# Causal attention with a channel mix: masks added after the score products, chunks 0 and 2 in one group, full-array spreads, a new order of all engines

## The chip, the cores and the metric

The kernel runs on one core of a Trainium2 chip. TensorE (PE in the rows, its weight loads PEld) multiplies matrices and writes to PSUM, VectorE (DVE), ScalarE (ACT) and GpSimd (POOL) do the elementwise work, and SyncE (SP) issues the transfers (DMA). The metric is the time of one execution on the device in microseconds, lower is better. The kernel before takes 474.48 us, the median of three runs (474.12 to 476.29).

## What is computed

Causal attention over 4 batches of 12 heads (448 positions, 64 values per head), then a channel mix on the joined heads (768 channels, 1024 inside):

```
scores = scale * q @ k.T ; scores[upper triangle] = -1e9
attn   = exp(scores - max) / (sum + 1e-9)
x      = (attn @ v) of all 12 heads side by side           # 4 x 448 x 768
xk = mu_k * x + (1 - mu_k) * x_prev ; xr = mu_r * x + (1 - mu_r) * x_prev
out = sigmoid(xr @ w_r) * (max(xk @ w_k, 0)**2 @ w_v)
```

`x_prev` is x one position earlier, zero at the start.

## The kernel before, in words

Two heads lie side by side on the 128 partitions: a pair w. There are 24 pairs, six to a batch. The 448 positions are cut into four chunks of 112. For chunk c of the queries, only keys up to chunk c are needed, so a row of scores has 112*(c+1) columns. The tiles of PSUM that hold scores (`s`, two buffers) hold several chunks: a **group** g, listed in `STEPS` (L389): chunks 0 and 1, chunk 2, chunk 3.

For one pair, in this order: `score` (L391) first writes the mask of the diagonal block into the group, as four matmuls of the identity `pick` with the triangle `mask` (L405; two halves h of a diagonal block, for two heads j), then adds the products of q and k (L418). The first six pairs multiply in full f32; from pair 6 on (`short`), q and k are split into a rounded part and a rest (`qk_hi`, `qk_lo`: tiles qh and ql), and three faster products are summed. The two heads j use rows 0 to 63 and 64 to 127 of the array, at the same time. `row_max` (L435, DVE) takes each row's maximum, one instruction for each chunk, `row_top` (L449 on DVE or L447 on ACT) turns it into a bias, `exps` (L458, ACT) takes the exponentials e and their sums. The weights e are then transposed: on TensorE for the first batch (`turn_e` L663, copied out by `copy_e` L674), later as two f16 parts p (`prob_hi` L639, `prob_lo` L643), turned by a DMA into pT. `weighted` (L705) multiplies them with v into the tile `bank`; this uses 64 columns of the array at a time. The reciprocals of the sums go through `turn_r` (L616) and `spread` (L626), and `evac` (L722) multiplies both into x. `mix_now`, `mix`, `mix_hi`, `mix_lo` (L249 to L255, L749, L756, L760) make xk and xr.

When six pairs are done, the batch's channel mix follows on TensorE: `mk` (xk times w_k, 8 outputs of 6 steps), `mr` (xr times w_r, 6 of 6) and `mv` (6 of 8), 448 columns at a time. For batch 0, mk and mr are full f32 matmuls (L981, two passes each, which the trace shows as two MATMULs); for the others a step is three f16 matmuls (L966). While one batch is mixed, the attention of the next one runs between its steps. For each batch some numbers are needed that are the largest over all partitions: `across` (L263) turns a column into a row (`turn`, tiles tp, L270), takes the maximum on DVE (`most`), and multiplies a 1x1 or 2x2 diagonal, tile `dg`, with a weight of ones to spread it to all partitions (`spread`, tiles bp, L281). The weight of this matmul has as many rows as numbers: 1 or 2. There are ten such spreads.

The three weight matrices come as 64-bit numbers, which are put together from two 32-bit halves: `w_z` (ACT, L840) reads the high half, `w_top` (POOL or ACT, L848, L850) the low one, `w_bits` (DVE, L854) joins them.

What runs in which order is written out by hand: each piece of work is a `plan.op`, and the table `starts` has a rank for every op; all instructions are issued in order of rank, so each engine's queue is in that order. The table `engines` says where an op that could run on ACT, DVE or POOL does run. `fills` puts matmuls into TensorE's queue whose result nothing uses (`idle`, L298), a pair of them for each unit, so many at this and that rank. An engine executes its queue in order; it waits for what an instruction needs.

The lines that the change touches:

Of the kernel before, what the change touches and what calls it, by code (L numbers as in the profile page):

```python
# [22 lines left out]
UP = 2.0**14  # L23
# [77 lines left out]
def tile_causal_attention_channel_mix(  # L101
# [73 lines left out]
    nc.vector.tensor_copy(pick[:D, 0], ident[:D, :CP])  # L175
    nc.vector.tensor_copy(pick[D:, 0, :D], ident[D:, D:])
    nc.vector.tensor_copy(pick[:D, 1, D:], ident[:D, : CP - D])
    nc.vector.tensor_copy(pick[D:, 1, D:], ident[D:, D:CP])
    nc.vector.tensor_copy(mask[:D], mask_up[:D])
    ident_h = const.tile([P, P], F16, name="identh")  # L180
# [22 lines left out]
    if "T" in CHOICE["pv"]:  # L203
        ident_b = early.tile([P, P], BF16, name="identb")
        nc.gpsimd.tensor_copy(ident_b, ident)
        mask_t = early.tile([P, 2, 1, CP], BF16, name="maskt")
        maskt_up = parted(x_ts[-2][:, 1 : 1 + CP])
        cleared(mask_t, maskt_up)
        triangles(mask_t, maskt_up, [[-D, 2], [0, 1], [1, CP]], -1, 0, masked)
        nc.vector.tensor_copy(mask_t[:D], maskt_up[:D])  # L210
        sel_m = early.tile([3 * N8, N8], BF16, name="selm")
        nc.gpsimd.memset(sel_m, 0.0)
        for i in range(3):
            nc.gpsimd.affine_select(
                out=sel_m, in_=sel_m, pattern=[[-1, N8]], compare_op=ALU.not_equal,
                fill=1.0, base=-N8 * i, channel_multiplier=1,
            )
        hot = early.tile([CP, NCH + 32], F32, name="hot")
        nc.gpsimd.memset(hot, 0.0)
        nc.gpsimd.memset(hot.rearrange("p (a c) -> p a c", c=NCH)[:, :, NCH - 1 :], 1.0)  # L220
        sel_t = early.tile([D, NCH, 2, D], F16, name="selt")
        nc.gpsimd.memset(sel_t, 0.0)
        nc.gpsimd.affine_select(
            out=sel_t, in_=sel_t, pattern=[[-1, NCH], [-32, 2], [0, D]], compare_op=ALU.not_equal,
            fill=1.0, base=0, channel_multiplier=1,
        )
        log_up = early.tile([P, 1], F32, name="logup")
        nc.gpsimd.memset(log_up, LOG_UP)
# [107 lines left out]

    def scaled_v(b, pv):
        s = p2.tile([P, 2], F32, tag="vsc", name=f"vsc_{b}")
        nc.vector.reciprocal(s[:, 0:1], pv)
        nc.vector.tensor_scalar(s[:, 1:2], s[:, 0:1], UP, None, ALU.mult)  # L340
        vsc[b] = (pv, s[:, 1:2])
        if plain(b, "k") and plain(b, "r"):
            nc.vector.tensor_scalar(shares_h, shares_p, pv, 1.0 / UP, ALU.mult, ALU.mult)

    def whole_p(w):

        return CHOICE["pv"][w] in "FT"

    def flipped(w):
        return CHOICE["pv"][w] == "T"  # L350
# [21 lines left out]
    def parts_v(w, i, e):  # L372
        s = vsc[w // NPAIR][1][:CP]
        src = vraw[w]
        if i == 0:
            vs[w] = p2.tile([CP, 2, 2 * NCH, D], F16, tag="vs", name=f"vs_{w}", bufs=NVS)
            scaled(vs[w][:, 0], src, s, e)
        elif e == "D":
            nc.vector.scalar_tensor_tensor(  # L379
                vs[w][:, 1], src, s, vs[w][:, 0], ALU.mult, ALU.subtract  # L380
            )
        else:
            scaled(src, src, s, e)
            tt[e](vs[w][:, 1], src, vs[w][:, 0], ALU.subtract)

    vmm, em, stat, sps, tot, sm = {}, {}, {}, {}, {}, {}


    STEPS = [{0: 0, 1: CP}, {2: 0}, {3: 0}]  # L389

    def score(w, g):  # L391

        s = ps_s.tile([P, 2, 512], F32, tag="s", name=f"s_{w}_{g}")
        sps[w, g] = s
        for h in range(2):
            for j in range(2):
                rows = slice(D * j, D * j + D)
                a = D * h
                if g == 0:
                    diagonal = s[:CP, j, :S].rearrange("p (a b) -> p a b", a=2)[:, :, a:CP]  # L400
                    fill = mask[rows, h, :, a:].to_broadcast([D, 2, CP - a])
                else:
                    (c,) = STEPS[g]
                    diagonal, fill = s[:CP, j, CP * c + a : CP * (c + 1)], mask[rows, h, 0, a:]
                nc.tensor.matmul(  # L405
                    diagonal, pick[rows, h], fill, start=h == 0, stop=False, skip_group_check=True
                )
# [31 lines left out]
    def most(w, g, a, z):  # L439
        a0 = min(STEPS[g])  # L440
        return sps[w, g][:CP, 0, S + 2 * (a - a0) : S + 2 * (z - a0)].rearrange("p (c j) -> p c j", j=2)
# [1097 lines left out]
```

## Time and profile before

| | |
|---|---|
| median of three runs | 474.48 us |
| the profiled execution's own time | 474.86 us |
| its span, first to last instruction | 473.1 us |
| granted TensorE clock, mean | 0.998 of full speed |
| busy: TensorE, DVE, ACT, POOL | 459.8, 353.8, 297.5, 178.3 us |

The span is 1.8 us shorter than the execution's time, for what lies before the first and after the last instruction. The table of stages (below) cuts the span at four places: the start of the first mk step (64.3 us), the last long wait of TensorE for ScalarE (118.4), and the start of the second batch's mk (193.6).

### The profile page before, as it was taken

The page shows a single profiled execution, that of the slowest core. Times are in us where ns is not written, and L with a number is a line of the kernel's source. Part 1 is how long each engine was busy: PE and PEld are TensorE (multiplying, and loading weights), DVE is VectorE, ACT ScalarE, POOL GpSimd, SP SyncE. Part 2 cuts the span into 40 slices and gives each one's busy share as a digit, 9 for nine tenths or more (in the row PEclk, how much of TensorE's full clock was granted, in tenths as well). Part 3 has the DMA queues.
Part 4 walks back from the last instruction along what each step waited for, and adds up shares of the span by engine and source line. Part 5 has one row for each costly group of instructions (what it writes and reads, how often), then busy time and mean ns, then how long its engine had stood idle before and what let it go on. Part 6 is the DMA issues. An engine that isn't in the chain of part 4 may idle for free.

```text
span 473.1 us, 9479 instructions
## 1 busy us (share of the span) xinstructions
PE 459.8 (97%) x3601; PEld 269.2 (57%) x3601; DVE 353.8 (75%) x722; ACT 297.5 (63%) x817; POOL 178.3 (38%) x177
## 2 busy tenths in 40 slices
PE   7989899999999899999999999999999999999996
PEld 5667655555465565555565666555665655555553
DVE  5899999898899988978797788775767784253211
ACT  5989889999949677578667544284578451223200
POOL 4424534414100433345323674237564542028200
PEclk9999999999999999999999999999999999999999
DMA  8787938573136658475156398363078673000002
GB/s 270 275 331 253 327 112 241 209 177 88 41 66 114 150 84 175 131 168 130 39 118 115 73 184 199 94 149 87 2 99 138 137 133 92 1 0 1 0 21 98
DMA packets 94846, 60.59 MB, mean 128 GB/s; under 512 B 83408, under 2 KB 86480, under 8 KB 94032
## 3 DMA queue, kind: packets, MB, share of 16 engines
q1 hardware_dynamic: 94800, 59.98, 50.5%
q8 instruction: 28, 0.46, 0.4%
q14 instruction: 18, 0.15, 0.1%
HBM read 33.82 MB, written 5.51 MB: 83 GB/s over the span
## 4 chain that ended last, share of the span: by engine, by line
PE 69%; DVE 4%; ACT 3%; DMA 1%; issue 1%; POOL 0%; DVEq 0%
PE mv L966 20%; PE mk L966 17%; PE mr L966 13%; PE bank L705 5%; PE s L418 5%; PE mr L981 5%; PE s L405 2%; DMA pT<-p 1%; ACT junk L806 1%; PE sp L626 1%; DVE s L435 1%; ACT e L458 1%; DVE vs L379 1%; POOL p L643 0%; DVE ql L369 0%
## 5 line engine op out<-in xcount | busy, mean ns | idle before, releaser
L966 PE MATMUL mv<-k,wv 128*128 128x448 f16 x576 | 113.2, 353 | 0.0
L458 ACT ACTIVATE e<-s,st 112x224 f32<-112x224 f32 (+3 forms) x192 | 92.9, 492 | 15.7 <-DVE st L449 12.3
L966 PEld LDWEIGHTS <-wv 128*128 128x128 f16 x576 | 54.7, 98 | 51.6 <-issue 2.9
L966 PE MATMUL mk<-xk,wk 128*128 128x448 f16 x432 | 83.4, 353 | 0.0
L435 DVE TENSOR_REDUCE s<-s 112x2 f32<-112x224 f32 (+3 forms) x96 | 70.5, 743 | 17.2 <-PE s L418 14.1
L966 PEld LDWEIGHTS <-wk 128*128 128x128 f16 x486 | 46.5, 98 | 44.4 <-issue 2.3
L966 PE MATMUL mr<-xr,wr 128*128 128x448 f16 x270 | 55.4, 353 | 0.0
L643 POOL TENSOR_TENSOR p<-e,p 112x1120 f16<-112x1120 f32 x15 | 36.7, 2447 | 48.2 <-DVE p L639 24.5
L966 PEld LDWEIGHTS <-wr 128*128 128x128 f16 x270 | 25.7, 98 | 23.6 <-issue 0.6
L458 ACT ACTIVATION_READ_ACCUMULATOR e<-s,st 112x1 f32 x192 | 38.9, 203 | 0.0
L981 PE MATMUL mk<-xk,wk 128*128 128x448 f32 x96 | 37.4, 544 | 0.0
L1076 DVE SCALAR_TENSOR_TENSOR a<-mv,kap,a 128x448 f32<-128x448 f32 x24 | 16.2, 678 | 24.7 <-PE mv L966 24.2
L643 DVE TENSOR_TENSOR p<-e,p 112x1120 f16<-112x1120 f32 x21 | 28.9, 1376 | 4.1 <-POOL p L639 3.6
L850 POOL TENSOR_SCALAR wraw<-wraw 128x768 int32<-128x768 uint16 (+1 forms) x19 | 23.3, 1228 | 22.7 <-DMA wraw<-in_w_k_dram 12.6
L705 PEld LDWEIGHTS <-vs 112*64 112x64 f16 x648 | 26.9, 110 | 6.0 <-issue 4.8
L705 PE MATMUL bank<-pT,vs 112*64 112x224 f16 (+1 forms) x648 | 29.7, 245 | 0.5 <-DMA pT<-p 0.5
L981 PE MATMUL mr<-xr,wr 128*128 128x448 f32 x72 | 29.3, 549 | 0.0
L749 DVE SCALAR_TENSOR_TENSOR xf<-xt,shares,xf 128x448 f32<-128x448 f32 x36 | 24.6, 686 | 5.7 <-ACT xf L249 5.4
L981 PEld LDWEIGHTS mk<-xk,wk 128*128 128x128 f32 x96 | 17.8, 190 | 17.4 <-issue 16.3
L639 ACT CAST p<-e 112x1120 f16<-112x1120 f32 x22 | 24.7, 1123 | 4.1 <-DMA pT<-p 4.0
L760 POOL TENSOR_TENSOR xr<-xf,xr 128x448 f16<-128x448 f32 x10 | 12.7, 1270 | 35.8 <-ACT xr L756 21.3
L447 ACT ACTIVATE st<-s 112x2 f32<-112x2 f32 (+1 forms) x37 | 6.2, 171 | 31.4 <-DVE s L435 27.5
(217 smaller groups left out, 850.3 us busy)
## 6 DMA issues: line engine op xcount, KB each, us to landing
qk<-in_qk_dram SPq DMA_DIRECT2D x24, 448.0 KB, 4.2
wraw<-in_w_k_dram SPq DMA_DIRECT2D x6, 1024.0 KB, 6.8
wraw<-in_w_v_dram SPq DMA_DIRECT2D x8, 768.0 KB, 5.2
vraw<-in_v_dram SPq DMA_DIRECT2D x24, 224.0 KB, 4.8
out_dram<-a SPq DMA_DIRECT2D x24, 224.0 KB, 2.4
wraw<-in_w_r_dram SPq DMA_DIRECT2D x6, 768.0 KB, 5.5
pT<-p SPq DMA_TRANSPOSE x36, 4.7
muT<-in_mu_dram SPq DMA_DIRECT2D x1, 6.0 KB, 8.6
```

Source lines behind the costliest of these rows:

```text
L418: nc.tensor.matmul(s[:CP, j, o : o + n], q_[rows, 0, c * CP : (c + 1) * CP], k_[rows, 1, :n], start=False, stop=c == max(STEPS[g]) and i = ...
L435: nc.vector.tensor_reduce(stat[w][:, c, :] if flipped(w) else most(w, g, c, c + 1), s[:CP, :, o : o + CP * (c + 1)], AX.X, ALU.max, negate ...
L458: nc.scalar.activation(em[w, j][:, blocks(c)].rearrange("p a b -> p (a b)"), sps[w, g][:CP, j, o : o + CP * (c + 1)], AF.Exp, bias=stat[w] ...
L639: copy[e](p_t[at_][:, :NB, :CP], em[w, j])
L643: tt[e](p[:, NB:, :CP], em.pop((w, j)), p[:, :NB, :CP], ALU.subtract)
L705: nc.tensor.matmul(px[w][64 * j : 64 * j + 64, cols], value(j, vi), p(j, pi), start=n == 0 and i == 0, stop=last and i == len(steps) - 1, ...
L749: nc.vector.scalar_tensor_tensor(f, x_of(w)[:, :S], share(w, mu, 1), f, ALU.mult, ALU.add)
L760: tt[e](t[:, 1], xf.pop((w, mu)), t[:, 0], ALU.subtract)
L850: nc.gpsimd.tensor_scalar(t, u, TOP3, -0.499, ALU.mult, ALU.add)
L966: nc.tensor.matmul(ps, w[:, wi, cols], x[:, xi, t0 : t0 + n], start=(i == 0 and a == 0), stop=(i == steps - 1 and a == 2),)
L981: nc.tensor.matmul(mps[m, kind, o][:, :n], z[:, o * P : (o + 1) * P], x, start=i == 0, stop=i == NO - 1)
L1076: nc.vector.scalar_tensor_tensor(s, mps.pop((m, "v", o))[:, : M[m][2]], kap[m][:, 3:4], s, ALU.mult, ALU.mult)
```

## The change

The groups become chunk 1; chunks 2 and 0 together; chunk 3. The products come first in a group, and the mask matmuls are added behind them. `pick` gets 128 columns instead of 112 (the last 16 are zero), so a mask matmul now writes all 128 partitions; for that, the first product of a chunk also takes 128 columns of q as its weight (the 16 that lie behind the chunk in memory; nothing reads these rows). In a group of two chunks, the products go chunk by chunk within each of the three summands. `across` multiplies with a weight of ones of all 128 rows; the diagonal lies in one of two tiles of 128x2 that are cleared once. `w_z` and `w_top` are told apart by halves of their tile, so that neither has to come before the other. The code of a way of working that no pair uses (`"T"`, `flipped`) goes. All three tables are new: 2161 ops have another rank, 722 choices of an engine are made anew, and the fills are 87 units instead of 111 (174 matmuls instead of 222, with one more at the start in both).

```
-    "fills": [[5,6],[95,16],[115,3],[255,13],[505,5],[535,4],...
+    "fills": [[15,12],[125,14],[215,9],[525,11],[615,3],[815,2],...
...
-    pick = const.tile([P, 2, CP], BF16, name="pick")
+    pick = const.tile([P, 2, P], BF16, name="pick")
...
+    diag = [const.tile([P, 2], F32, name=f"diag{i}") for i in range(2)]
+    for t in diag:
+        nc.gpsimd.memset(t, 0.0)
...
-            st["dg"] = p2.tile([P, 2], F32, tag="dg", name=f"dg_{nm}")
+            st["dg"] = diag[len(spreads) % 2]
...
-                st["bp"][:, :n], ones[:n].to_broadcast([n, P]), st["dg"][:n, :n], start=True, stop=True
+                st["bp"][:, :n], ones.to_broadcast([P, P]), st["dg"][:, :n], start=True, stop=True
...
-    STEPS = [{0: 0, 1: CP}, {2: 0}, {3: 0}]
+    STEPS = [{1: 0}, {2: 0, 0: 3 * CP}, {3: 0}]
+    PLACE = {c: i for i, c in enumerate(c for g in STEPS for c in g)}
...
-        for h in range(2):
-            for j in range(2):
-                rows = slice(D * j, D * j + D)
-                a = D * h
-                if g == 0:
-                    diagonal = s[:CP, j, :S].rearrange("p (a b) -> p a b", a=2)[:, :, a:CP]
-                    fill = mask[rows, h, :, a:].to_broadcast([D, 2, CP - a])
-                else:
-                    (c,) = STEPS[g]
-                    diagonal, fill = s[:CP, j, CP * c + a : CP * (c + 1)], mask[rows, h, 0, a:]
-                nc.tensor.matmul(
-                    diagonal, pick[rows, h], fill, start=h == 0, stop=False, skip_group_check=True
-                )
...
-        for c, o in STEPS[g].items():
-            n = CP * (c + 1)
-            for i, (q_, k_) in enumerate(products):
+        top = max(STEPS[g])
+        for i, (q_, k_) in enumerate(products):
+            for c, o in STEPS[g].items():
+                n = CP * (c + 1)
                 for j in range(2):
-                    rows = slice(64 * j, 64 * j + 64)
+                    rows = slice(D * j, D * j + D)
+                    wide = P if i == 0 else CP
                     nc.tensor.matmul(
-                        s[:CP, j, o : o + n],
-                        q_[rows, 0, c * CP : (c + 1) * CP],
+                        s[:wide, j, o : o + n],
+                        q_.rearrange("p a s -> p (a s)")[rows, c * CP : c * CP + wide],
                         k_[rows, 1, :n],
-                        start=False,
-                        stop=c == max(STEPS[g]) and i == len(products) - 1,
+                        start=i == 0 and c == top,
+                        stop=False,
                         skip_group_check=True,
                     )
+        for h in (1, 0):
+            for j in range(2):
+                rows = slice(D * j, D * j + D)
+                a, z = D * h, CP * len(STEPS[g])
+                diagonal = s[:, j, CP * top : CP * top + z].rearrange("p (a b) -> p a b", b=CP)[:, :, a:]
+                fill = mask[rows, h, :, a:].to_broadcast([D, len(STEPS[g]), CP - a])
+                nc.tensor.matmul(
+                    diagonal, pick[rows, h], fill, start=False, stop=h == 0, skip_group_check=True
+                )
...
-        plan.op("ACT", scalar(w) + 85, w_z, (n,), [(st, None, "r"), (z, None, "w")])
-        plan.op({"ACT": scalar(w) + 85, "POOL": 1.24 * w + 110}, 0, w_top, (n,), [(st, None, "w")])
+        plan.op("ACT", scalar(w) + 85, w_z, (n,), [(st, "h", "r"), (z, None, "w")])
+        plan.op({"ACT": scalar(w) + 85, "POOL": 1.24 * w + 110}, 0, w_top, (n,), [(st, "l", "w")])
```

On TensorE, a group of one chunk (here chunk 3 of the pair that is scored just ahead of the first mk step) reads before like this, where `s` is the group's tile, and "x2" a matmul for each head:

```order
L405 LDWEIGHTS pick
L405 MATMUL s_2_1156<-mask,pick 112x112
...
L405 MATMUL s_2_1156<-mask,pick 112x48
L418 MATMUL s_2_1156<-ql_1034,qh_1032 112x448 x2
L418 MATMUL s_2_1156<-qh_1032,ql_1034 112x448 x2
L418 MATMUL s_2_1156<-qh_1032 112x448 x2
L981 MATMUL mk_0_1203<-xk_682,wk 128x448
```

On TensorE, a group of chunk 3 of the same pair now (L384 is `score`'s product, L398 its mask):

```order
L384 MATMUL s_2_1070<-ql_999,qh_924 128x448 x2
L384 MATMUL s_2_1070<-qh_924,ql_999 112x448 x2
L384 MATMUL s_2_1070<-qh_924 112x448 x2
L398 LDWEIGHTS pick
L398 MATMUL s_2_1070<-mask,pick 128x48
...
L398 MATMUL s_2_1070<-mask,pick 128x112
```

The four masks have gone behind the products, and the narrower half comes first.

On TensorE, around the first mk steps of batch 0 (xk_682 and so on are the inputs of pairs 0, 1, ...; mk_0, mk_1 outputs), it was:

```order
L418 MATMUL s_2_1156<-qh_1032 112x448 x2
L981 MATMUL mk_0_1203<-xk_682,wk 128x448
L981 MATMUL mk_0_1203<-xk_877,wk 128x448
L981 MATMUL mk_0_1203<-xk_959,wk 128x448
L981 MATMUL mk_0_1203<-xk_1122,wk 128x448
L981 MATMUL mk_0_1203<-xk_1174,wk 128x448
L705 MATMUL bank<-pT_0_1099,vraw_957 64x224
```

On TensorE at the same place (L828 is the f32 step, L463 `turn_r`, L473 `spread`, L510 `turn_e`, L552 `weighted`), now:

```order
L510 MATMUL eT_1_2_1092<-ident,e_1_889 112x112 x4
L463 LDWEIGHTS rs_136
L463 MATMUL rp_1101<-identh,rs_136 128x112
L828 MATMUL mk_0_1103<-xk_585,wk 128x448
L828 MATMUL mk_0_1103<-xk_697,wk 128x448
L828 MATMUL mk_1_1120<-xk_585,wk 128x448
L828 MATMUL mk_1_1120<-xk_697,wk 128x448
L473 LDWEIGHTS sel
L473 MATMUL sp_1128<-rt_1125,sel 128x112
```

The mix starts when the inputs of two pairs are there, with two outputs at a time; eleven steps, not five, stand ahead of the next pair's scores, among the last steps of pairs 4 and 5.

On DVE, the first reductions of the program (s_0 is pair 0's first group; "x2" is two instructions, L179 the end of the mask's making) were:

```order
L179 COPY mask<-xt_95 64x224
L435 TENSOR_REDUCE s_0_171<-s_0_171 112x2 x2
L435 TENSOR_REDUCE s_1_187<-s_1_187 112x2
L449 TENSOR_SCALAR st_180<-s_1_187 112x2
L435 TENSOR_REDUCE s_2_242<-s_2_242 112x2
```

On DVE at the start of the program (L410 `row_max`, L423 `row_top`), now:

```order
L179 COPY mask<-xt_95 64x224
L410 TENSOR_REDUCE s_0_189<-s_0_189 112x2
L423 TENSOR_SCALAR st_196<-s_0_189 112x2
L410 TENSOR_REDUCE s_1_204<-s_1_204 112x2 x2
L423 TENSOR_SCALAR st_196<-s_1_204 112x4
```

The first group has one reduction where it had two, and the second one two.

## Rows read from the trace of the kernel before

**Rows 1.** Busy time by stage: start:end, length, each engine's busy us (instructions), clock, DMA.

```profile
0.00:64.30 64.30, 57.87 (x702) 41.53 (x702) 54.77 (x114) 54.53 (x169) 28.94 (x47) 1.00 0.80 276
64.30:118.40 54.10, 53.10 (x244) 28.33 (x244) 50.41 (x115) 50.43 (x143) 18.00 (x13) 1.00 0.61 171
118.40:193.60 75.20, 73.03 (x608) 43.20 (x606) 68.89 (x149) 55.77 (x142) 19.37 (x14) 1.00 0.52 109
193.60:473.10 279.50, 275.85 (x2057) 156.13 (x2055) 179.69 (x348) 136.75 (x365) 112.02 (x105) 1.00 0.42 91
```

**Rows 2.** TensorE's waits from 64.3 to 193.6: waiter, releaser, us, times, longest.

```profile
PE rp L616 <- DVE xt L636: 1.6, 1, 1.6
PE s L405 <- ACT e L458: 0.9, 1, 0.9
PE bank L705 <- DMA pT<-p: 0.5, 1, 0.5
```

**Rows 3.** Timeline of TensorE, 247 to 263 us: start, us, line, operands, rows*columns, shape, count.

```profile
248.71 0.28 PE L405 MATMUL s<-mask,pick 64*112 64x112 bf16 x4
248.84 0.44 PE L418 MATMUL s<-ql,qh 64*112 64x448 f32 x2
...
249.62 0.74 PE L966 MATMUL mr<-xr,wk 128*128 128x448 f16 x3
...
250.96 3.00 PE L966 MATMUL mr<-xr,wr 128*128 128x448 f16 x15
253.80 6.41 PE L966 MATMUL mv<-k,wv 128*128 128x448 f16 x33
260.13 1.64 PE L705 MATMUL bank<-pT,vs 112*64 112x224 f16 x36
```

**Rows 4.** Timeline of TensorE, 328 to 336 us.

```profile
328.41 0.27 PE L270 MATMUL tp_k<-ident,kmm 128*1 128x128 f32 x1
328.52 0.73 PE L966 MATMUL mr<-xr,wr 128*128 128x448 f16 x3
...
329.75 0.38 PE L281 MATMUL bp_k<-dg_k,ones 1*128 1x1 f32 x2
330.06 3.58 PE L966 MATMUL mr<-xr,wr 128*128 128x448 f16 x18
...
333.67 0.35 PE L405 MATMUL s<-mask,pick 64*112 64x224 bf16 x4
333.83 0.29 PE L418 MATMUL s<-ql,qh 64*112 64x112 f32 x2
333.96 0.26 PE L418 MATMUL s<-qh,ql 64*112 64x112 f32 x2
334.05 0.26 PE L418 MATMUL s<-qh 64*112 64x112 f32 x2
...
334.51 0.23 PE L405 MATMUL s<-mask,pick 64*112 64x112 bf16 x4
334.59 0.39 PE L418 MATMUL s<-ql,qh 64*112 64x336 f32 x2
334.82 0.32 PE L418 MATMUL s<-qh,ql 64*112 64x336 f32 x2
...
335.22 0.38 PE L281 MATMUL bp_v<-dg_v,ones 1*128 1x1 f32 x2
```

**Rows 5.** TensorE by line and shape: count, busy us, mean ns, idle before.

```profile
L298 PE MATMUL bank<-busy 128*128 128x64 f16 x222 | 10.4, 198 | 0.0
```

**Rows 6.** Timeline of all engines, the first scores, 3 to 7 us.

```profile
5.46 1.07 DVE L435 TENSOR_REDUCE s<-s 112x2 f32<-112x224 f32 x2 [2.35 <-PE s L418]
...
6.83 0.45 ACT L458 ACTIVATE e<-s,st 112x224 f32<-112x224 f32 x1
```

**Rows 7.** DVE and POOL by line and shape.

```profile
L369 DVE TENSOR_TENSOR ql<-qk,qh 128x896 fp32r<-128x896 f32 x16 | 17.7, 1104 | 2.4 <-ACT qh L364 1.2 <-POOL qh L364 1.2
L369 POOL TENSOR_TENSOR ql<-qk,qh 128x896 fp32r<-128x896 f32 x2 | 5.0, 2482 | 6.5 <-ACT qh L364 6.5
```

More of the change, by code (lines that the diff above doesn't have):

```diff
@@ L97 @@
+    "fills": [[15,12],[125,14],[215,9],[525,11],[615,3],[815,2],[1045,3],[1205,2],[1255,1],[1505,2],[1545,2],[1605,1],[1735,1],[1845,1],[1975,3],[2185,9],[2285,3],[2325,1],[2365,2],[2865,3],[2925,2]],
 }
@@ L202, in tile_causal_attention_channel_mix @@
     N8 = 2 * NCH
[L203 to L216, printed above, removed]
-            )
[L218 to L228, printed above, removed]
+    diag = [const.tile([P, 2], F32, name=f"diag{i}") for i in range(2)]
+    for t in diag:
+        nc.gpsimd.memset(t, 0.0)
+    spreads = []
     rs_t = []
@@ L486, in copy_m @@
-    def copy_m(w, e):
-        mt[w] = early.tile([3 * N8, CP], BF16, tag="mt", name=f"mts_{w}", bufs=2)
-        copy[e](mt[w], pst.pop(w)[: 3 * N8, :CP])
-    def score_t(w, g):
-        s = ps_s.tile([P, 2, 512], F32, tag="s", name=f"st_{w}_{g}")
-        spt[w, g] = s
-        for i, o in enumerate(FLIPPED[g].values()):
-            for h in range(2):
-                for j in range(2):
-                    rows = slice(D * j, D * j + D)
-                    nc.tensor.matmul(
-                        s[:CP, j, o : o + CP], pick[rows, h], mask_t[rows, h, 0],
-                        start=i == 0 and h == 0, stop=False, skip_group_check=True,
-                    )
-        for kb, o in FLIPPED[g].items():
-            for j in range(2):
-                rows = slice(64 * j, 64 * j + 64)
-                nc.tensor.matmul(
-                    s[:CP, j, o : o + S - kb * CP],
-                    qkt[w][rows, 1, kb * CP : (kb + 1) * CP],
-                    qkt[w][rows, 0, kb * CP :],
-                    start=False, stop=False, skip_group_check=True,
-                )
@@ L511, in score_m @@
-    def score_m(w, g):
-        s = spt[w, g]
-        for kb, o in FLIPPED[g].items():
-            for c in range(kb, NCH):
-                for j in range(2):
-                    nc.tensor.matmul(
-                        s[:CP, j, o + (c - kb) * CP : o + (c - kb + 1) * CP],
-                        sel_m[:, 2 * c + j : 2 * c + j + 1].to_broadcast([3 * N8, CP]),
-                        mt[w],
-                        start=False,
-                        stop=kb == max(FLIPPED[g]) and c == NCH - 1,
-                        skip_group_check=True,
-                    )
@@ L568, in spread_t @@
-    def spread_t(w):
-        sm[w] = ps_t.tile([P, 512], F32, tag="t", name=f"sp_{w}")
-        t = rt.pop(w)
-        for c in range(NCH):
-            for i in range(2):
-                nc.tensor.matmul(
-                    sm[w][:, c * CP : (c + 1) * CP],
-                    sel_t[:, c].rearrange("k j d -> k (j d)"),
-                    t[:, i],
-                    start=c == 0 and i == 0,
-                    stop=c == NCH - 1 and i == 1,
-                    skip_group_check=True,
-                )
@@ L582, in weighted_t @@
-    def weighted_t(w):
-        px[w] = bank
-        for kb in range(NCH):
-            for j in range(2):
-                nc.tensor.matmul(
-                    px[w][64 * j : 64 * j + 64, kb * CP : S],
-                    vraw[w][:, j * NCH + kb, :],
-                    em[w, j].rearrange("p a b -> p (a b)")[:, START_OF[kb] : START_OF[kb] + S - kb * CP],
-                    start=kb == 0,
-                    stop=kb == NCH - 1,
-                    skip_group_check=True,
-                )
@@ L1197, in scores @@
             )
-            if flipped(w):
-                continue
             plan.op({"ACT": 210, "DVE": 160}, 0, row_top, (w, g), [(s, None, "r"), (ts_, g, "w")])
-            for c in chunks if not flipped(w) else ():
+            for c in chunks:
                 for j in range(2):
@@ L1442, in more_weights @@
             "NONE", 0, swap, ("kr", ["wv", "v"]),
-            [((f"w{n}", 0, 1), None, "r") for n in range(2 * NO)] + [(("late_v", 0, 1), None, "w")]
-            + [(x_tile(w), None, "r") for w in range(NPAIR) if flipped(w)],
+            [((f"w{n}", 0, 1), None, "r") for n in range(2 * NO)] + [(("late_v", 0, 1), None, "w")],
         )
@@ L1456, in attend @@
                 pair(w)
-            if w + 1 in ws and not flipped(w) and not short(w + 1):
+            if w + 1 in ws and not short(w + 1):
                 pair(w + 1)
@@ L1461, in attend @@
                 after_scores(w - 1)
-            if w + 1 in ws and flipped(w) and not short(w + 1):
-                pair(w + 1)
         after_scores(ws[-1])
```

126 lines of the change are left out of this document (15 added, 111 removed).

## The prediction

> **What bounds the kernel now.** I read the stages first. From 193.6 us on, TensorE is the only limit: it is busy for 275.85 of 279.5 us, while DVE has 179.69 and ACT 136.75 of work [rows 1], and the list of TensorE's waits is empty for this stretch; the 3.6 us that are missing are the last output's way out. From 64.3 to 193.6 us TensorE waits three times, 3.0 us in all [rows 2]. In the first 64.3 us it is busy for 57.87, but partly with fills, and ACT and DVE have 54.5 us each [rows 1]: there the chain from scores to x, on these two engines, sets the pace. From 64.3 to 118.4 all three are close to full: TensorE 53.10, DVE 50.41, ACT 50.43 of 54.1 us. So what TensorE no longer has to do counts in full after 193.6 us, and mostly between 64.3 and 193.6; what DVE and ACT do earlier or later counts in the first 118 us. The granted clock is at its full level in every stage, so it is no term.
>
> The new order does not trade work between the stages: from the first three-pass mk step of batch 1 to the end, TensorE's queue holds the same instructions in both kernels (1188 big matmuls, 432 of pv, 120 score products, 120 masks, 48 of sp, 5 spreads). The stretch of 279.5 us therefore carries over, less what each instruction saves, if no wait comes into it.
>
> **Part 1: changes of the array's rows and columns.** Fifteen mr matmuls, followed by more of their kind, take 253.80 - 250.96 = 2.84 us, 0.189 each. The 33 mv behind them, followed by pv on 64 columns, take 260.13 - 253.80 = 6.33 us where 33 x 0.189 = 6.24: the change costs 0.09 us [rows 3]. The weight load behind such a change is not hidden. I counted the places in both queues after the first mk step where neighbours differ in rows or columns (full, the 64 rows of scores, the 64 columns of pv, the 1 or 2 rows of the spreads): 105 before, 87 now. Twelve of the 18 lie behind 193.6 us (62 and 50). The ten spreads are the main reason: with 128 rows they no longer differ from the mr beside them. 18 x 0.09 = **1.6 us**, 1.1 of it in the last stage.
>
> **Part 2: the spread itself.** The two passes of bp take 330.06 - 329.75 = 0.31 us, of which 0.09 is the change behind them, counted above [rows 4]. With all rows the first load hides behind an mr; two f32 loads remain, and the nearest row, tp, takes 0.11 for one pass [rows 4]. So 0.11 to 0.22 instead of 0.22; I take 0.18: 10 x 0.04 = **0.4 us** (0 to 1.1).
>
> A rule of the Trainium skill speaks against both parts. Rows first: full-array matmuls with a new weight each follow each other at 0.189 us, so their loads do overlap [rows 3]. "TensorE: Matmul & The Clock Gate" (Part 3, The mechanism) says that a weight load overlaps with running matmuls only when the two use different row groups; by it a spread on all rows would conflict with its neighbours, parts 1 and 2 would bring nothing, and the sum would be 2.0 us poorer. The trace does not bear it out here.
>
> **Part 3: the masks.** The columns that stream are the same, 160 for a chunk. What differs is which loads stand open. Before, the masks hold up the products: in an opening group by 0.16 us plus the 0.03 by which the first product's row is longer (0.29 against 0.26); in a second group by 0.08 plus 0.07 (0.39 against 0.32) [rows 4]; in a lone group by 0.13 [rows 3] plus about 0.07. For a pair in two visits: 0.19 + 0.15 + 0.20 = 0.54. Now each visit opens with a product's load. With 112 columns the products of chunk 0 come every 0.09 to 0.10 us, though they stream for half of that [rows 4]: that is the load, so 0.11 with 128 columns. Behind the first group 0.03 for the narrow mask and 0.11 for the next load, behind the second 0.14 for masks of 96 and 224 columns, behind the lone one 0.08; 0.05 comes back since the last product of chunk 0 now has a mask's load behind it. 0.11 + 0.14 + 0.14 - 0.05 + 0.11 + 0.08 = 0.53. The result lies within what I can resolve; by whole blocks (1.55 for two groups [rows 4], 0.91 for one [rows 3]) the same parts give 0.06 less. I take 0.03 x 18 pairs = **0.5 us**, between -0.9 and +1.8. The six f32 pairs lie where TensorE has time.
>
> The masks also lengthen the way from a group's product to its maximum, by about 0.08 us; it matters only where DVE waits for scores, in the first stage.
>
> **Part 4: the first 118 us.** The first exponential starts at 6.83 us, after two reductions that take 1.07 from 5.46 [rows 6]. The new first group has one chunk: one reduction instead of two and fewer products, but masks behind. Estimate: 0.4 + 0.5 - 0.2 = 0.7 us earlier. Then eleven mk steps, not five, stand ahead of pair 7's scores, in a place where TensorE used to run fills or wait; six steps of two passes are 4.5 us of TensorE's work done early. The fills removed (48 of 222, of 10.4 us busy [rows 5]) are time in which TensorE had nothing to do, so worth nothing themselves. But the work of DVE and ACT up to the end of batch 0's mk is the same in both orders within 2 to 3 us when I add up the queues by their rows, and from 64.3 to 118.4 DVE has only 54.1 - 50.4 = 3.7 us to spare [rows 1]. So the early steps gain at most these 3.7 and the 0.7, 4.4 us, and at least nothing. An order made anew can also lose: a few waits like the three of [rows 2], 3.0 us. I take **2.0 us**, between -3 and +4.4; the middle, because the stage is nearly full on three engines.
>
> `w_top` next to `w_z`, and fewer instructions on DVE later (11 ql instead of 16), lie beside TensorE's work: nothing. If that cover went, they would be worth a few us.
>
> **The sum.** 1.6 + 0.4 + 0.5 + 2.0 = 4.5 us. The profiled execution has a span of 473.1 and a time of 474.86, so 470.4; the median of the runs is 0.4 below it: **470.1 us**. A measurement of this kernel can tell about 0.5% from no change, that is 472.1 to 476.9.
>
> **Rivals.**
>
> The new order pays in full: all 4.4 us of part 4, and the masks at their good end (1.8): 1.6 + 0.4 + 1.8 + 4.4 = 8.2, **466.3 us**. For it: TensorE starts on mk with two pairs. Against: DVE and ACT would have to run without a gap for 50 us.
>
> DVE stays the limit up to 193.6 us: nothing comes of part 4, nor of what parts 1 to 3 save before that; then 1.1 + 0.2 + 0.3 = 1.6 us remain, **472.9 us**, no change. For it: DVE is at 92% from 64.3 to 193.6 (119.3 of 129.3 [rows 1]) and its work there does not shrink.
>
> Parts 1 and 2 bring nothing, since the full-array loads stand as open as the others: **472.1 us**, at the edge. Against it [rows 3]. The rule of the Trainium skill in part 2 ("TensorE: Matmul & The Clock Gate", Part 3, The mechanism) would lead here.
>
> Slower: POOL is late. Seven splits ql run on POOL instead of two, 2.48 us each against 1.10 on DVE [rows 7], and eleven instead of seven first parts of p. The products of a short pair wait for ql, and everything queued behind them on TensorE, mk and mv steps too, waits as well. If the five moved splits each come 1.4 us late, TensorE waits 7 us: 474.5 - 4.5 + 7 = **477.0 us**. It decides from the point where a split lands less than 1.4 us before its scores' turn. Against: POOL is busy for 112 of the last 279.5 us [rows 1], and today no split keeps TensorE waiting there.
>
> **How the numbers follow.** Forecast 0.50; the full gain 0.13; DVE the limit 0.19; the loads open 0.05; POOL late 0.13. Faster by over 0.5%: 0.50 + 0.13 = 0.63. Within: 0.19 + 0.05 = 0.24. Slower: 0.13. The range: the low end below the full gain, 465.0, since its bounds add up there; the high end 476.5, which takes in the limit by DVE and half of the slow case.
>
> **What will show it.** In the profile after, bp beside mr should cost under 0.2 us from its start to the next mr's, with 0.189 ahead of it. From batch 1's first mk to the end there should be 277.4 to 278 us with no waits of TensorE; a wait of a score product for ql on POOL there means the slow case. Batch 1's mk should start at about 191 us; if it starts at 193.6 or later, part 4 was wrong, and DVE should then be over 92% busy up to there. Masks that come more than 0.1 us after the last product's end would make part 3 wrong. Wrong as a whole is the prediction if new waits of more than 3 us stand ahead of mk steps.

## The result and the profile after

The changed kernel takes 468.37 us, the median of four runs (468.12 to 469.28); the kernel before took 474.83 beside it. The ratio is 0.9847, with a 95% interval of 0.9819 to 0.9876: faster by 1.5%, where the prediction had 0.9%. The time lies in the predicted range, 1.7 us under the predicted 470.1. The profiled execution took 468.12 us, with a span of 466.4.

The stages of the kernel after, cut as in [rows 1] at the first mk step and at the second batch's (start:end, length, busy us of PE, PEld, DVE, ACT and POOL with their instructions, clock, DMA share and GB/s):

```profile
0.00:63.70 63.70, 57.27 (x646) 41.50 (x646) 52.97 (x110) 51.71 (x163) 34.19 (x50) 1.00 0.76 268
63.70:188.40 124.70, 124.70 (x856) 71.69 (x853) 115.11 (x256) 108.56 (x294) 38.21 (x35) 1.00 0.58 151
188.40:466.40 278.00, 274.32 (x2061) 156.37 (x2055) 182.63 (x348) 141.52 (x375) 106.62 (x94) 1.00 0.36 89
```

The three stretches were 64.3, 129.3 and 279.5 us long; they lost 0.6, 4.6 and 1.5 us. The middle one is where the prediction fell short; batch 1's mk starts at 188.4 us, where about 191 was announced. In that stretch TensorE is now busy for every one of the 124.70 us. All its waits in the whole execution (waiter, releaser, us, times, longest):

```profile
PE bank L277 <- DVE xt L569: 1.5, 1, 1.5
PE s L384 <- DMA qk<-in_qk_dram: 1.4, 1, 1.4
PE eT L510 <- DVE pT L521: 1.1, 3, 0.5
PE bank L273 <- DVE busy L148: 1.1, 1, 1.1
PE eT L510 <- ACT e L432: 0.5, 2, 0.3
PE rp L463 <- ACT xt L483: 0.2, 1, 0.2
```

Every one of them lies ahead of 63.7 us. The three waits of [rows 2], 3.0 us, are gone, and none has come in their place.

DVE had 54.77 + 50.41 + 68.89 = 174.1 us of work ahead of the second batch's mk [rows 1] and has 168.1 now; POOL had 66.3 and has 72.4. In the middle stretch DVE is still at 92% (115.11 of 124.70), as it was.

A spread of the kernel after stands among mr steps like this (timeline of TensorE: start, us, line, operands, rows*columns, shape, count):

```profile
322.62 0.73 PE L813 MATMUL mr<-xr,wr 128*128 128x448 f16 x3
323.18 0.37 PE L260 MATMUL bp_k<-diag,ones 128*128 128x1 f32 x2
323.42 1.29 PE L813 MATMUL mr<-xr,wr 128*128 128x448 f16 x6
```

Three mr and the spread take 323.42 - 322.62 = 0.80 us; without the 3 x 0.189 of the mr that is 0.23. Not every spread costs the same. Four of the ten take only 0.14 us up to the next matmul, the other six 0.21 to 0.24; what makes the difference, no run shows. One of the four:

```profile
327.49 0.28 PE L260 MATMUL bp_v<-diag,ones 128*128 128x1 f32 x2
327.63 0.73 PE L813 MATMUL mr<-xr,wk 128*128 128x448 f16 x3
```

### The profile page after: what moved, and what is told of

Its sections match the earlier page's. It is cut to its first block, busy times and chain, and to the rows that moved or that the text cites. A ratio compares the mean times of both kernels' runs of the same rounds, so it can differ in the third digit from the quotient of the medians.

```text
span 466.4 us, 9442 instructions
## 1 busy us (share of the span) xinstructions
PE 456.3 (98%) x3553; PEld 269.6 (58%) x3553; DVE 350.7 (75%) x712; ACT 301.8 (65%) x829; POOL 179.0 (38%) x178
## 4 chain that ended last, share of the span: by engine, by line
PE 91%; DVE 5%; ACT 1%; issue 1%; DMA 1%; POOL 1%; DVEq 0%; POOLq 0%; ACTq 0%
PE mv L813 24%; PE mk L813 18%; PE mr L813 13%; PE s L384 10%; PE mk L828 8%; PE bank L552 7%; PE mr L828 6%; DVE s L410 2%; PE eT L510 2%; PE s L398 2%; PE sp L473 1%; DVE pT L521 1%; DVE wk L701 1%; ACT e L432 1%; DMA qk<-in_qk_dram 1%
## 5 line engine op out<-in xcount | busy, mean ns | idle before, releaser
L432 ACT ACTIVATE e<-s,st 112x224 f32<-112x224 f32 (+3 forms) x192 | 93.1, 494 | 25.9 <-DVE st L423 21.4
L410 DVE TENSOR_REDUCE s<-s 112x2 f32<-112x448 f32 (+2 forms) x96 | 71.4, 745 | 23.8 <-PE s L398 20.6
L490 POOL TENSOR_TENSOR p<-e,p 112x1120 f16<-112x1120 f32 x13 | 31.6, 2436 | 20.5 <-DVE p L486 7.2
L828 PE MATMUL mk<-xk,wk 128*128 128x448 f32 x96 | 37.9, 546 | 0.0
L490 DVE TENSOR_TENSOR p<-e,p 112x1120 f16<-112x1120 f32 x23 | 32.6, 1417 | 0.1
L828 PE MATMUL mr<-xr,wr 128*128 128x448 f32 x72 | 29.8, 550 | 0.0
L552 PE MATMUL bank<-pT,vs 112*64 112x224 f16 (+1 forms) x648 | 29.5, 245 | 0.0
L552 PEld LDWEIGHTS <-vs 112*64 112x64 f16 x648 | 26.8, 110 | 4.1 <-issue 2.1
L828 PEld LDWEIGHTS mk<-xk,wk 128*128 128x128 f32 x96 | 17.7, 190 | 16.0 <-issue 14.8
L836 ACT ACTIVATE a<-mk 128x448 f32<-128x448 f32 x22 | 11.8, 538 | 23.1 <-PE mk L813 22.8
L697 POOL TENSOR_SCALAR wraw<-wraw 128x768 int32<-128x768 uint16 (+1 forms) x15 | 17.4, 1158 | 24.0 <-DMA wraw<-in_w_v_dram 13.3
L486 ACT CAST p<-e 112x1120 f16<-112x1120 f32 x20 | 22.4, 1123 | 3.2 <-DMA pT<-p 3.1
L908 ACT COPY a<-mr 128x448 f32<-128x448 f32 x19 | 10.1, 530 | 21.9 <-PE mr L813 20.3
```

What stands on the lines that cost most here:

```text
L410: nc.vector.tensor_reduce(most(w, g, i, i + 1), s[:CP, :, o : o + CP * (c + 1)], AX.X, ALU.max, negate=True)
L432: nc.scalar.activation(em[w, j][:, blocks(c)].rearrange("p a b -> p (a b)"), sps[w, g][:CP, j, o : o + CP * (c + 1)], AF.Exp, bias=stat[w] ...
L486: copy[e](p_t[at_][:, :NB, :CP], em[w, j])
L490: tt[e](p[:, NB:, :CP], em.pop((w, j)), p[:, :NB, :CP], ALU.subtract)
L552: nc.tensor.matmul(px[w][64 * j : 64 * j + 64, cols], value(j, vi), p(j, pi), start=n == 0 and i == 0, stop=last and i == len(steps) - 1, ...
L697: nc.gpsimd.tensor_scalar(t, u, TOP3, -0.499, ALU.mult, ALU.add)
```

## The experiments

Three theories stood at the beginning. A: the new instructions save about 2.5 us, as in parts 1 to 3, and the rest is the new order. B: in the old order DVE sets the pace up to batch 1's mk, so there the instructions save nothing before it. C: the new instructions themselves took the waits away. A further question followed: is it the order of the queues, or the choice of engines, that removes the waits?

### Order and instructions apart

`new_instr` is the kernel before with its groups and tables, and with full-array spreads and masks behind the products, which run chunk by chunk within each summand as in the changed kernel:

```
-    pick = const.tile([P, 2, CP], BF16, name="pick")
+    pick = const.tile([P, 2, P], BF16, name="pick")
...
-        for c, o in STEPS[g].items():
+            for c, o in sorted(STEPS[g].items(), reverse=True):
...
-                st["bp"][:, :n], ones[:n].to_broadcast([n, P]), st["dg"][:n, :n], start=True, stop=True
+                st["bp"][:, :n], ones.to_broadcast([P, P]), st["dg"][:, :n], start=True, stop=True
```

> The kernel before, with its groups, its three tables and so its order, but with the new instructions: masks of 128 columns behind the products, and spreads on all rows. Theory A (the new instructions save 1.5 us behind the second batch's mk and about 1 us before it, the new order saves the other 4 us): 472.0 us, the last stage 277.9 to 278.1 us long, TensorE's three waits between 64.3 and 193.6 us still there, 3 us in all. Theory B (DVE sets the pace up to the second batch's mk in this order): mk of batch 1 starts at 193.6 as before, 472.9 us. Theory C (the instructions themselves are what removed the three waits): 469 us or less.

Measured: 472.88 us, 0.9957 (0.9939 to 0.9975) of the kernel before. Its first mk step comes at 65.0 us. Its two later stages and, below them, TensorE's waits from 65 us on:

```profile
65.00:192.60 127.60, 124.75 (x850) 71.02 (x845) 118.97 (x262) 106.69 (x285) 37.45 (x27) 1.00 0.52 137
192.60:471.00 278.40, 274.83 (x2059) 155.43 (x2055) 180.40 (x348) 136.85 (x365) 112.44 (x105) 1.00 0.38 91
```

```profile
PE rp L623 <- DVE xt L643: 1.7, 1, 1.7
PE s L413 <- ACT e L465: 1.2, 1, 1.2
```

`old_instr` is the opposite: the changed kernel with its tables, its groups and its order of products, but masks of 112 columns ahead of the products, and spreads on 1 or 2 rows:

```
-                st["bp"][:, :n], ones.to_broadcast([P, P]), st["dg"][:, :n], start=True, stop=True
+                st["bp"][:, :n], ones[:n].to_broadcast([n, P]), st["dg"][:n, :n], start=True, stop=True
...
+        for h in (0, 1):
...
+                    diagonal, pick[rows, h, :CP], fill, start=h == 0, stop=False, skip_group_check=True
...
-        for h in (1, 0):
```

> The changed kernel with its order, but with the masks of 112 columns ahead of the products and with spreads on 1 or 2 rows, as before. Theory A: 468.4 + 2.5 = 470.9 us, no new waits of TensorE behind 64 us, the second batch's mk at 189.4 us. Theory C: the three waits come back, 473 to 474 us.

Measured: 470.20 us, 0.9890 (0.9872 to 0.9908), with no wait of TensorE behind 63 us:

```profile
63.00:188.80 125.80, 125.80 (x856) 71.74 (x853) 115.33 (x256) 108.70 (x294) 38.44 (x35) 1.00 0.58 149
188.80:467.60 278.80, 275.17 (x2059) 156.75 (x2055) 182.96 (x348) 141.78 (x375) 106.19 (x94) 1.00 0.38 88
```

Theory A holds, C falls: with the old order the two larger waits stay whatever the instructions are, and with the new order they are gone, with the old instructions too. Theory B named 472.9 us, and the median of new_instr lies there; against the kernel before beside it, its gain of 0.4% fits A's 2.5 us and B's 1.6 alike. The stages decide: the stretch between the two mk is 1.7 us shorter than before (127.6 against 129.3), which B excludes. From the first mk step to the end, the kernel before takes 408.8 us (473.1 - 64.3), the new order alone 404.6, the new instructions alone 406.0, both 402.7. So the order is worth 4.2 us with the old instructions, and the instructions 1.9 us on top of it; alone, in the old order, they are worth 2.8. These are differences of one trace each; by all runs the order gives 1.1%, the instructions in the old order 0.4%, both together 1.5%. The stage ahead of the first mk step took between 63.0 and 64.6 us in four kernels that share the new order (after, old_instr and, below, masks_ahead and one_pass); what a kernel gains or loses there, under a us, these runs can't tell. (one_choice, further below, is the kernel before up to 154 us, and it has its first mk step at 63.7 us instead of 64.3.)

### Masks and spreads apart

`masks_ahead` is the changed kernel with only the masks put back ahead of the products, with 112 columns (the second and third change of old_instr).

> The changed kernel with its order, groups and spreads, but with masks of 112 columns ahead of the products. From the four runs so far (masks behind: first mk step 0.67 us later, later stages 0.06 us dearer each; spreads: 1 us cheaper in each of the last two stages): 0.8 us less than the changed kernel, 467.6 us; first mk step at 63.0 us, and behind it 124.7 and 274.2 us. If the masks behind the products do save 0.5 us, as predicted: 468.9 us.

Measured: 468.58 us, 0.9858 (0.9844 to 0.9873):

```profile
64.00:188.70 124.70, 124.70 (x855) 71.64 (x853) 115.21 (x256) 108.54 (x294) 38.17 (x35) 1.00 0.58 148
188.70:466.60 277.90, 274.24 (x2059) 156.51 (x2055) 182.67 (x348) 141.59 (x375) 105.93 (x94) 1.00 0.38 89
```

The stretches are 124.7 and 277.9 us long, against 124.7 and 278.0 with the masks behind: the place of the masks is worth nothing in this order. (The 274.2 of the expectation is TensorE's busy time in the last stage, not its length.) The 0.8 us expected rested on a first mk step at 63.0 us, which old_instr had by chance; here it came at 64.0. The spreads alone are the difference to old_instr: 404.6 - 402.6 = 2.0 us, 0.2 for each of the ten. Where they come from is seen in the same place in old_instr:

```profile
323.24 0.73 PE L813 MATMUL mr<-xr,wr 128*128 128x448 f16 x3
323.90 0.38 PE L260 MATMUL bp_k<-diag,ones 1*128 1x1 f32 x2
324.21 1.31 PE L813 MATMUL mr<-xr,wr 128*128 128x448 f16 x6
```

Three mr and the spread take 0.97 us here and 0.80 in the kernel after. The three mr ahead take 0.66 instead of 0.56: the change of rows costs 0.10 in front of the spread. The spread itself takes 0.31 instead of 0.24.

`one_pass` goes on from there. The numbers spread are powers of two, so bf16 holds them exactly, and one pass replaces two:

```
-    busy = const.tile([P, P], F16, name="busy")
+    busy = const.tile([P, P], BF16, name="busy")
...
-    diag = [const.tile([P, 2], F32, name=f"diag{i}") for i in range(2)]
+    diag = [const.tile([P, 2], BF16, name=f"diag{i}") for i in range(2)]
...
-                st["bp"][:, :n], ones.to_broadcast([P, P]), st["dg"][:, :n], start=True, stop=True
+                st["bp"][:, :n], busy, st["dg"][:, :n], start=True, stop=True
```

> As masks_ahead, and the ten spreads in one bf16 pass (their numbers are powers of two) instead of two f32 passes. If the price of a spread is its passes and f32 weight loads, each goes from 0.14 to about 0.06 us: 0.8 us less than masks_ahead, 466.8 us. If it is what stands open beside it, no change against masks_ahead.

Measured: 467.98 us, 0.9844 (0.9827 to 0.9860). The same place again:

```profile
323.16 0.73 PE L813 MATMUL mr<-xr,wr 128*128 128x448 f16 x3
323.73 0.17 PE L260 MATMUL bp_k<-diag,busy 128*128 128x1 bf16 x1
323.76 1.67 PE L813 MATMUL mr<-xr,wr 128*128 128x448 f16 x8
```

Three mr and the spread now take 0.60 us; the spread costs 0.03. The ten spreads together are 1.6 us shorter by their rows (0.1 to 0.2 each), but the trace behind the first mk step is only 0.8 us shorter (401.8 against 402.6); why, no run shows. The fills are bf16 here too, since they use the same tile `busy`. The median is 0.6 us under masks_ahead, inside the intervals of both. It is the lowest median here, and no measured gain over the changed kernel's 0.9847.

### Order or choice of engine?

`old_engines` is the changed kernel with the string of 722 choices of the kernel before; `new_engines` the kernel before with the new string. Nothing else differs.

> The changed kernel with the choices of engines of the kernel before (722 entries); order and instructions stay. DVE then gets back some 6 us of work that POOL does now ahead of the second batch's mk. Theory D (the order of the queues removed the waits, the engines only follow): 468.4 to 469.5 us, waits of TensorE behind 64 us under 1 us. Theory E (the 6 us less on DVE removed them): waits of 3 us or more come back, 471.4 us or more.

> The kernel before with the changed kernel's choices of engines alone; its order and instructions stay. Theory D: the waits stay, 474.5 us or more, since the choices were made for another order. Theory E: the three waits of 3.0 us go, 471.5 us.

Measured: 567.15 us, 1.1933 (1.1904 to 1.1961), and 557.19 us, 1.1714 (1.1677 to 1.1751). The span of old_engines is 565.7 us, that of new_engines 551.2. Busy time from their pages, in this order:

```profile
PE 488.0 (86%) x3553; PEld 281.9 (50%) x3553; DVE 371.5 (66%) x722; ACT 298.0 (53%) x817; POOL 182.4 (32%) x179
```

```profile
PE 486.9 (88%) x3601; PEld 279.3 (51%) x3601; DVE 374.9 (68%) x712; ACT 303.9 (55%) x829; POOL 186.9 (34%) x176
```

Both theories fall. The spans grow by 99 and 78 us over those of the kernels that they come from. DVE is busy for 21 us more in both, TensorE for 32 and 27, ACT and POOL for at most 9. In old_engines TensorE stands idle for 78 us (565.7 - 488.0), where the changed kernel has 10. The reading that fits, not tested operation by operation: an instruction that another engine executes comes at a place in that engine's queue where its input isn't there yet, and holds up what stands behind it. In old_engines the engines wait for each other, for instance ACT for DVE (the first of these groups has 13.0 us in the changed kernel, the second 21.4):

```profile
ACT st L421 <- DVE s L410: 43.2, 23, 6.3
ACT e L432 <- DVE st L423: 30.1, 15, 6.2
```

TensorE's mean granted clock is lower too, 0.946 in old_engines and 0.957 in new_engines, where the kernels that they come from have 1.00. Order and choices are one table in two pieces, so the question has to be put to few choices at a time.

### One choice

In the kernel before, the longest wait of [rows 2] ends with DVE's copy at 158.2 us. DVE and, below it, POOL ahead of it (timeline of the kernel before):

```profile
154.46 2.81 DVE L379 SCALAR_TENSOR_TENSOR vs<-vraw,vsc,vs 112x512 f16<-112x512 f32 x1
157.19 0.15 DVE L610 TENSOR_TENSOR rs<-su,rs 112x8 f16<-112x8 f32 x1
157.26 1.05 DVE L435 TENSOR_REDUCE s<-s 112x2 f32<-112x224 f32 x2
158.22 0.61 DVE L636 COPY xt<-sp 128x448 f32<-128x448 f32 x1
```

```profile
154.06 2.66 POOL L643 TENSOR_TENSOR p<-e,p 112x1120 f16<-112x1120 f32 x1 [4.54 <-ACT p L639]
```

DVE's instruction took 2.81 us, where the median of the 14 of its kind is 0.74. It ended 0.55 us after POOL's (157.27 against 156.72), so most of its usual 0.74 us came when POOL's had ended. The Trainium skill says why ("SBUF — State Buffer", Who interferes with whom): a DVE instruction with two inputs in SBUF and a POOL instruction that reads SBUF need the same port, and the one that comes second stands still until the first has done. This row agrees: the two inputs are vraw and vs, both in SBUF.

`one_choice` changes one letter of the kernel before: this POOL instruction goes to DVE. `one_back` makes the reverse change in the changed kernel, which has it on DVE.

> The kernel before with one choice of engine changed: the second part of p of pair 9 (head 1), which POOL computes from 154.06 to 156.72 us, goes to DVE, at the same rank. In that time DVE's second part of v, which has both inputs in SBUF, took 2.81 us instead of 0.74, and TensorE waited 1.6 us for the copy behind it. Theory F (POOL's instruction held DVE's, and the wait counts in full, since TensorE is the limit from there on): this wait goes, 1.6 us less than the kernel before, 473.2 of 474.8. Rival (DVE is the limit up to the second batch's mk, its 1.3 us more make up for it): no change, a wait comes later.

> The reverse of one_choice: the changed kernel with the second part of p of pair 9 (head 1) on POOL, as before, instead of DVE (where it takes 1.33 us from 152.05), at its new rank. DVE's next instruction, the second part of v of pair 9, has both inputs in SBUF. Theory F: it is held until POOL has done, it takes about 2.3 us or more instead of 0.75, which is all that DVE has saved; the waits on TensorE stay under 1 us, since nothing queued close behind is awaited: 468.4 us, within 0.5. If a hold of this kind alone had cost the kernel before its 1.6 us: 470 us.

Measured, one_choice: 475.37 us, 1.0002 (0.9988 to 1.0016), no change. DVE and POOL in one_choice, and TensorE's waits behind 63.7 us:

```profile
153.87 0.74 DVE L379 SCALAR_TENSOR_TENSOR vs<-vraw,vsc,vs 112x512 f16<-112x512 f32 x1
...
159.10 2.75 DVE L749 SCALAR_TENSOR_TENSOR xf<-xt,shares,xf 128x448 f32<-128x448 f32 x1
```

```profile
158.91 2.45 POOL L643 TENSOR_TENSOR p<-e,p 112x1120 f16<-112x1120 f32 x1 [9.97 <-ACT p L639]
```

```profile
PE mv L966 <- DVE a L1076: 1.3, 1, 1.3
PE s L405 <- ACT e L458: 0.9, 1, 0.9
PE bank L705 <- DMA pT<-p: 0.7, 1, 0.7
```

The cause of the wait is confirmed: without POOL's instruction, DVE's takes its 0.74 us and the wait of rp is gone. That its end would be a gain is not: POOL's next instruction of this kind catches another of DVE's with two inputs, which takes 2.75 us, and TensorE waits 1.3 us for DVE a little later. TensorE's waits add up to 2.9 us, as before to 3.0.

Measured, one_back: 468.72 us, 0.9855 (0.9835 to 0.9875), no change either, as theory F has it. DVE and POOL there:

```profile
152.53 0.61 DVE L607 TENSOR_TENSOR xk<-xf,xk 128x448 f16<-128x448 f32 x1
153.27 2.35 DVE L229 TENSOR_SCALAR vs<-vraw,vsc 112x512 f16<-112x512 f32 x1
```

```profile
152.03 3.30 POOL L490 TENSOR_TENSOR p<-e,p 112x1120 f16<-112x1120 f32 x1 [0.68 <-DVE p L486]
```

It is another instruction than I expected that is held: a TENSOR_SCALAR with one input, 2.35 us where the kernel after takes 0.48 in the same place. The one I expected, with two inputs, had begun at 151.87, ahead of POOL's, and took its 0.74. Nothing that TensorE needs stood close behind it.

### Sixteen choices

`dve_back` takes 16 operations between the first mk step and the second batch's from POOL back to DVE, where the kernel before has them (splits of weights, of q and k, of p, of v, of x and of the sums); `pool_more` makes the same 16 moves the other way in the kernel before.

> The changed kernel with 16 operations between the first mk step and the second batch's mk moved from POOL back to DVE, where the kernel before has them; order and all other choices stay. By the rows of DVE they are 10.2 us of work there; DVE has 9.6 of 124.7 us free in that stretch. Theory G (the gain between 64 and 193 us came from what DVE no longer has to do): the second batch's mk comes 2 to 4 us later, TensorE waits for DVE, 470.5 to 472.5 us. Rival (the order alone): 468.4 us, no waits.

> The kernel before with the same 16 operations moved from DVE to POOL; order and all other choices stay. Theory G: TensorE's waits between 64.3 and 193.6 us go, 3 us less than the kernel before, 471.8 us. Rival (a choice of engine only pays together with the order made for it, since POOL takes twice as long and holds DVE's instructions with both inputs in SBUF): waits for POOL, slower than the kernel before by more than 2 us.

Measured: dve_back 481.20 us, 1.0122 (1.0092 to 1.0151); pool_more 483.93 us, 1.0168 (1.0131 to 1.0206). The stretch between the two mk in dve_back, and in pool_more:

```profile
65.80:201.10 135.30, 127.61 (x856) 72.20 (x853) 122.75 (x270) 108.25 (x292) 19.60 (x18) 0.99 0.54 139
```

```profile
67.10:201.20 134.10, 126.61 (x847) 71.58 (x845) 122.62 (x247) 106.75 (x285) 61.22 (x45) 1.00 0.53 130
```

In dve_back DVE has 7.6 us more to do (122.75 against 115.11), and the stretch is 10.6 us longer. TensorE, which had no wait there, now has 7.6 us of them, the two largest:

```profile
PE s L384 <- ACT e L432: 3.0, 3, 1.6
PE tp_v L248 <- DVE vmm L313: 2.3, 1, 2.3
```

Theory G was right in direction and far too small: DVE is free for 9.6 of 124.7 us, but not where these operations stand. The rival, that the order alone removed the waits, falls.

In pool_more DVE has 16 instructions less to do, worth 10 us, and yet it is busy for 122.62 us instead of 119.3. For this I compared each DVE instruction with two inputs in SBUF that starts within an instruction of POOL in this stretch with the shortest of its form, and added up what it took more. Kernel before: 8 such instructions, 2.9 us, of which 2.1 are the one at 154.46. pool_more: 19, 13.0 us. Kernel after: 3, under 0.1 us. So the 10 us that DVE no longer computed it stood still for POOL; that gives 119.4, and the last 3 us up to 122.62 this count doesn't explain. Theory G falls here. In the changed kernel DVE's instructions with two inputs hardly meet POOL's. That the same choices pay there for this reason fits, but no run shows it apart from the order.

### The fills

`no_fills` is the changed kernel with an empty table of fills.

> The changed kernel without its 174 fills. If the fills only stand in time in which TensorE has nothing to do, as the prediction has it: 468.4 us, within 0.5. Rival: they keep TensorE's clock at its full level; then the granted clock falls in the first 64 us, the matmuls there take twice as long, and the time grows by some us.

Measured: 473.37 us, 0.9953 (0.9927 to 0.9979) of the kernel before, 5.0 us more than the changed kernel, and less steady (470.4 to 476.2). The transposes of no_fills at four places:

```profile
15.64 0.81 PE L510 MATMUL eT<-ident,e 112*112 112x112 f32 x3
...
18.30 1.55 PE L510 MATMUL eT<-ident,e 112*112 112x112 f32 x7
...
21.17 0.50 PE L510 MATMUL eT<-ident,e 112*112 112x112 f32 x3
...
23.46 0.88 PE L510 MATMUL eT<-ident,e 112*112 112x112 f32 x7
```

Seven transposes take 1.55 us at 18.3 and 0.88 at 23.5. From three to seven, the four more cost 0.74 us at the first two places, 0.185 each, and 0.38 at the last two, 0.095 each. So TensorE ran at half the rate until about 20 us. In the kernel after, three take 0.48 at 10.39, so there the full rate is reached at 10 us:

```profile
10.39 0.48 PE L510 MATMUL eT<-ident,e 112*112 112x112 f32 x3
```

The granted clock reads 1.00 in both kernels and doesn't show this, so in these traces a reading of 1.00 in the first 20 us is no sign of the full rate. The first mk step comes 1.7 us later (65.4). The slow start can explain this; but kernels with the same order and all fills differ by 1.6 us there. The other us come behind it: TensorE waits for DVE three times, 3.0 us in all, the longest 1.7 for a step of mv. Why these waits come, no run shows.

## Where the prediction was right and where not

**What bounds the kernel.** Right. From batch 1's mk to the end there is no wait and the stretch is 278.0 us long, where 277.4 to 278 were announced. Of the 1.5 us, the spreads bring 0.9 (278.8 in old_instr, 277.9 in masks_ahead). About 0.7 is there with the old instructions too (279.5 to 278.8), 0.5 of it in the score blocks of the new groups (below), which the prediction had put down to the masks.

**Parts 1 and 2, 1.6 + 0.4 us.** Right in the sum: the spreads brought 2.0 us in both stages together, which is what the two parts have. Not right in the split. The rows showed an exit of 0.09 us [rows 3]; the entry in front of the spread costs another 0.10 with the old spread, and the announced sign, under 0.2 us from bp to the next mr, came at four of the ten spreads (0.14), not at the others (0.21 to 0.24). The rival by which full-array loads stand open and nothing is gained fell: the rule of the Trainium skill weighed there ("TensorE: Matmul & The Clock Gate", Part 3, The mechanism) is contradicted by the 0.97 and 0.80 us above.

**Part 3, 0.5 us for the masks.** Wrong in the new order: nothing (masks_ahead). The price of the open loads was taken from the kernel before with its groups. In the last stage the score blocks take 24.47 us before and 24.08 in new_instr, so there the 0.4 us are found; but they take 24.01 with the masks ahead in the new groups and 24.07 with them behind (sums of TensorE's rows from start to start). The new groups gave it already.

**Part 4, 2.0 us for the first 118.** This is the term that was mis-sized: the order brought 4.2 us behind the first mk step. The first exponential came 0.6 us earlier (6.21 against 6.83 us), where 0.7 was estimated; of this and of the first mk step, 0.6 us earlier, no gain in time can be told, since that step moves by as much between kernels that are alike up to there. Of the 4.2 us, 3.5 lie in the middle stretch (129.3 to 125.8 in old_instr): TensorE's 3.2 us of idle time there are gone, and its work is 0.3 shorter. That 4.2 lies so near the stated bound of 4.4 is chance. The bound was DVE's spare time ahead of 118.4 us, and 2.2 of the 3.2 us of idle time lay behind it (75.20 - 73.03 [rows 1]), where the prediction expected nothing of the order. It set new waits against the gain and took the middle, because the stage is nearly full on three engines; no new wait came, and the three old ones went. Whether the early mk steps had a part in this, no run shows. What I did not read in the trace was why the longest wait was there: DVE's instruction of 2.81 us beside POOL's stood in the timeline, and so did the sum of such holds, 2.9 us. That DVE's work up to batch 1's mk would not shrink was wrong too; it fell by 6.0 us, 4.2 of them in the middle stretch, and 2.8 of those are these holds.

**The sum.** Its terms give 470.0 us, not 470.1 (474.86 - 4.5 - 0.4). That it came within 1.7 us owes something to luck: the 0.5 us of part 3, which the masks did not bring, made up for some of what part 4 had too little.

**The rivals.** "DVE stays the limit" fell for the changed kernel. For the old order it is half right: one_choice took a wait away and gained nothing, but the new instructions did shorten the stretch between the two mk (127.6 against 129.3 in new_instr). "POOL is late" fell: no wait of TensorE behind 63.7 us. What it feared, POOL in DVE's way, is real and shows in pool_more, 8 us slower.

**The fills.** "Worth nothing themselves" holds for the 48 that were removed at most, and no run removes them alone; without any the kernel loses 5.0 us. The prediction took a granted clock of 1.00 in every stage as the reason that the clock is no term; no_fills shows half the rate under the same reading.

What stays open: how much of the 4.2 us is the order of the queues, the groups, the choices of engine, the fills, or the loosened order of `w_z` and `w_top`. Order and choices swapped singly don't work; the others no run takes apart, but for the 0.5 us of the score blocks.

## What to carry to other kernels

Where queues are ordered by hand, as here, a table of engine choices and a table of ranks can be worth something only together; test moves a few at a time, and expect a removed wait to reappear at the next place where two engines meet. Before costing work moved from DVE to POOL by its duration, look at which DVE instructions will run beside it: those that need the same port can take as long as POOL's. A small matmul between large ones costs more than what it computes: of the 0.40 us of a one-row spread, 0.17 went with the change of rows (0.97 to 0.80) and 0.20 with the two f32 passes (0.80 to 0.60).

## What the runs showed of the hardware

- A spread on one row between full-array matmuls costs 0.40 us (0.97 - 3 x 0.189), on all rows 0.23 in the same place and 0.14 in four others, in one bf16 pass 0.03.
- A TENSOR_SCALAR with one input in SBUF was held by POOL as well: 2.35 us instead of 0.48, until 0.3 us after POOL's instruction ended (155.62 against 155.33). The page "SBUF — State Buffer" of the Trainium skill (Who interferes with whom) lists this operation among those that can take the shared port; the row agrees.
- POOL seems to be held too, when it comes second: its instruction in one_back took 3.30 us, where the kernel after has a mean of 2.44 for this form, while DVE's one beside it ran in 0.61.
- Without fills TensorE ran at half rate until about 20 us (0.185 us for a transpose, 0.095 later), though the granted clock read 1.00 and it had been busy for 11.1 of the 12 us from 8 to 20.
